# Weight rounding in single operations over two batches, attention units in twos, and a gated block by columns first

## The chip, the core and the metric

The kernel runs on one core of a Trainium2 chip. The metric is the device time of one execution in microseconds; the time before is the median of three runs. The engines work beside each other, each through its own queue in order: TensorE (PE) does matrix products, with its weight loads shown apart as PEld; VectorE (DVE) and ScalarE (ACT) work element by element; GpSimd (POOL) and SyncE (SP) here issue transfers between device memory and the on-chip memories. An engine waits where an operand isn't there or a buffer isn't free.

## The reference

Attention by hash buckets, then a gated feed-forward block on its result:

```
B, H, S, D = 4, 8, 768, 64
q_bits = (einsum('bhsd,dk->bhsk', q, proj) > 0)          # 6 bits
k_bits = (einsum('bhsd,dk->bhsk', k, proj) > 0)
mask   = bucket(q_bits) == bucket(k_bits)                # 2**arange(6)
scores = where(mask, q @ k.T / sqrt(D), -1e9)
attn   = exp(scores - max); attn /= attn.sum(-1) + 1e-9
x      = (attn @ v) as (B*S, H*D) = (3072, 512)
g      = x @ w_gate;  val = x @ w_val                    # 512 -> 1536
out    = (g * sigmoid(g) * val) @ w_out                  # 1536 -> 512
```

q, k, v and proj come as 32-bit floats. The three weight matrices come as 64-bit floats and reach the chip as pairs of 32-bit words.

## The kernel before

**Units.** Two heads of one batch make a pair; there are 16 pairs, four to a batch. A pair has 12 units: two halves of the 768 queries (384 each), and for each half six chunks `c` of 128 keys. `score(u)` (L209) computes, for both heads, keys by queries: two bf16 matmuls of the hash bits, then four instructions of the f32 product, into a tile `sc` with two buffers. The bits are scaled so that equal buckets add zero and others a very large negative number (`OFF` is 2**35). ScalarE takes the exponential (L219) into one of four ring tiles `A`. `attend(u)` (L221) multiplies by v into the accumulator `av`, and VectorE sums the exponentials of the chunks in `acc` (L232, L235). After the sixth chunk ScalarE copies `av` out (L238), and `norm` (L240) sums `acc` over partitions with a matmul into `sum`, takes the reciprocal on VectorE (L251 to L255) and writes a part of `xT`, the input of the gated block.

**Front.** `front(n)` (L170) gives eight steps for a pair: four transposes of q or k on TensorE (`tps`), copied by ScalarE (L182), and four matmuls with `proj2` (`hps`, L187), whose signs VectorE turns to bits (L189), with one more multiply for k (L192). A constant column in `proj2` carries the offset that makes the agreement of all bits sum to zero.

**Weights.** 36 pieces of 128 x 512 doubles are rounded to f32 by integer operations on VectorE: `narrow(i)` (L143) issues seven operations for one piece, through a scratch tile `x`, and then asks GpSimd for the words of piece i + 2 (L141). The first 24 pieces are those of the gate and value weights, in three groups of 512 columns; the last 12 are those of `w_out`.

**Gated block.** When the last normalization of a batch is issued, `push_ffn(b)` (L264) appends 72 closures, here called atoms. `up` (L271) makes 8 matmul instructions into `g` or `val`; for `g` ScalarE does a tanh (L279) and VectorE combines (L280), for `val` VectorE makes `ht` (L285). `down` (L289) does three of twelve steps of the output product into `po` (one buffer), and after the twelfth ScalarE copies it to `o` (L298) and SP writes the rows out. The order is one half of the columns at a time: 24 `up`, then 12 `down`, then the same for the second half.

**Order.** The order on each engine is the order in which the program issues the instructions; nothing is reordered by a planner. One loop (L317) runs over units: `score(u)`, one front step of the next pair where `at >= 2`, one whole `narrow(u)` for the first 36 units, a load of the pair after next at the last unit of a pair, then atoms, of which a credit of 72/44 = 1.64 accrues per unit, then `attend(u - 1)`, then `norm` of unit u - 3 if it closed a half. What is left of the atoms follows the loop.

**Buffers that are shared.** `bank(...)` (L70) gives out two PSUM buffers in turn, for `tps`, `hps`, `sum`, `g` and `val` alike. `po` and `av` have one buffer each, `sc` two of two banks.

Of the kernel before, what the change touches and what calls it, by code (L numbers as in the profile page):

```python
# [17 lines left out]
def kernel(  # L18
# [23 lines left out]
    NF = DF // P  # L42
    PIECE = 512
# [26 lines left out]
    def bank(name):  # L70
        return mm_ps.tile([P, 512], FP32, tag="mm", name=name)
# [5 lines left out]
    def load(n):  # L77
        b, pr = pairs[n]
        for name, src in (("q", q), ("k", k)):
            t = raw.tile([P, NCH, 2, D], FP32, tag=name + "raw", name=name + "raw")  # L80
            for h in range(2):
                nc.sync.dma_start(t[:, :, h, :],
                                  src[b, 2 * pr + h].rearrange("(p c) d -> p c d", c=NCH))
            raws[name, n] = t
        t = raw.tile([P, 2, NCH, D], FP32, tag="vraw", name="vraw", bufs=3)
        nc.sync.dma_start(
            t.rearrange("p h c d -> p h (c d)"),
            v[b, 2 * pr : 2 * pr + 2].rearrange("h (p c) d -> p h (c d)", c=NCH),
        )
        raws["v", n] = t  # L90
# [1 line left out]
    load(0)  # L92


    proj2 = konst.tile([P, P], FP32, tag="proj2", name="proj2")
    nc.vector.memset(proj2, 0.0)
    for o in (0, D):
        nc.sync.dma_start(proj2[o : o + D, o + 1 : o + 1 + NBITS], proj[:, :])
    shift = {}
    for name, one in (("q", -1.0), ("k", 0.25 * NBITS)):  # L100
        t = konst.tile([P, 1], FP32, tag="shift" + name, name="shift" + name)
        nc.vector.memset(t, 0.0)
        for o in (0, D):
            nc.vector.memset(t[o : o + 1 + NBITS], 0.5)
            nc.vector.memset(t[o : o + 1], one)
        shift[name] = t
    ident = konst.tile([P, P], FP32, tag="ident", name="ident")
    make_identity(nc, ident)
    ones = konst.tile([P, D], FP32, tag="ones", name="ones")
# [25 lines left out]
        pieces.append((wo[:, f, :], moe_w_out[f * P : (f + 1) * P, :]))  # L135
    words = {}

    def load_words(i):
        if i < len(pieces):
            words[i] = wraw.tile([P, PIECE, 2], I32, tag="words", name="words")  # L140
            nc.gpsimd.dma_start(words[i].rearrange("p f w -> p (f w)"), pieces[i][1])  # L141

    def narrow(i):  # L143
        t = words.pop(i)
        lo, hi = t[:, :, 0], t[:, :, 1]
        w = pieces[i][0]
        wi = w.bitcast(I32)
        x = wraw.tile([P, PIECE], I32, tag="x", name="x")
        nc.vector.tensor_scalar(wi, hi, scalar1=3, scalar2=0x3FFFFFFF,
                                op0=ALU.logical_shift_left, op1=ALU.bitwise_and)  # L150
        nc.vector.scalar_tensor_tensor(out=wi, in0=hi, scalar=-(1 << 30), in1=wi,
                                       op0=ALU.bitwise_and, op1=ALU.bitwise_or)
        nc.vector.scalar_tensor_tensor(out=wi, in0=lo, scalar=29, in1=wi,
                                       op0=ALU.logical_shift_right, op1=ALU.bitwise_or)
        nc.vector.tensor_scalar(x, lo, scalar1=28, scalar2=1,  # L155
                                op0=ALU.logical_shift_right, op1=ALU.bitwise_and)
        nc.vector.tensor_tensor(wi, wi, x, op=ALU.add)  # L157
        nc.vector.tensor_single_scalar(x, hi, 0x7FFFFFFF, op=ALU.bitwise_and)  # L158
        nc.vector.scalar_tensor_tensor(out=w, in0=x, scalar=float(897 << 20), in1=w,
                                       op0=ALU.is_ge, op1=ALU.mult)  # L160
        load_words(i + 2)

    for i in range(2):
        load_words(i)


    T = {}
# [2 lines left out]
    def front(n):  # L170
# [13 lines left out]
        def hash_bits(name, half):  # L184
            cols = slice(half * HQ, (half + 1) * HQ)
            ps = bank("hps")
            nc.tensor.matmul(ps[:, 0:HQ], proj2, T[name, n][:, cols], start=True, stop=True)  # L187
            o = bits[name, n][:, cols]
            nc.vector.tensor_scalar(o, ps[:, 0:HQ], scalar1=0.0, scalar2=shift[name],  # L189
                                    op0=ALU.is_gt, op1=ALU.subtract)  # L190
# [30 lines left out]
    def attend(u):  # L221
# [12 lines left out]
        elif c > 1:  # L234
            nc.vector.tensor_tensor(acc[n, half], acc[n, half], a[:, :, 0:HQ], op=ALU.add)  # L235
        if c == NCH - 1:
            av[n, half] = att.tile([P, AW], FP32, tag="avs", name="avs")
            nc.scalar.copy(av[n, half], ps[:, 0:AW])  # L238

    def norm(u):  # L240
# [6 lines left out]
        for h in range(2):  # L247
            nc.tensor.matmul(ps[h * D : (h + 1) * D, 0:HQ], ones, t[:, h, :], start=True, stop=True)  # L248
        a = av.pop((n, half))
        r = att.tile([P, HQ], FP32, tag="r", name="r")  # L250
        nc.vector.tensor_scalar(r, ps[:, 0:HQ], scalar1=S * EPS, scalar2=None, op0=ALU.add)  # L251
        nc.vector.reciprocal(r, r)  # L252
        e = att.tile([P, 1], FP32, tag="e", name="e")
# [9 lines left out]

    def push_ffn(b):  # L264
        x = xT.pop(b)
        for half in range(2):
            cols = slice(half * HQ, (half + 1) * HQ)
            hs = []
            now = {}

            def up(f, w, name, x=x, cols=cols, now=now, hs=hs):  # L271
                ps = bank(name)
                for j in range(NJ):
                    nc.tensor.matmul(ps[:, 0:HQ], w[:, j, f * P : (f + 1) * P], x[:, j, cols],  # L274
                                     start=j == 0, stop=j == NJ - 1)

                if name == "g":
                    t = ffn.tile([P, HQ], FP32, tag="t", name="t")
                    nc.scalar.activation(t, ps[:, 0:HQ], AF.Tanh, scale=0.5)  # L279
                    nc.vector.scalar_tensor_tensor(out=t, in0=t, scalar=1.0, in1=ps[:, 0:HQ],  # L280
                                                   op0=ALU.add, op1=ALU.mult)
                    now["t"] = t
                else:
                    ht = hp.tile([P, HQ], FP32, tag="ht", name="ht")
                    nc.vector.scalar_tensor_tensor(out=ht, in0=now["t"], scalar=0.5,  # L285
                                                   in1=ps[:, 0:HQ], op0=ALU.mult, op1=ALU.mult)
                    hs.append(ht)

            def down(i, fs, now=now, hs=hs, half=half):  # L289
                if fs[0] == 0:  # L290
                    now["o"] = po_ps.tile([P, DM], FP32, tag="po", name="po")
                ps = now["o"]
                for f in fs:
                    nc.tensor.matmul(ps, hs[f][:, i * P : (i + 1) * P], wo[:, f, :],  # L294
                                     start=f == 0, stop=f == NF - 1)
                if fs[-1] == NF - 1:
                    o = ffn.tile([P, DM], FP32, tag="o", name="o")
                    nc.scalar.copy(o, ps)  # L298
                    rows = out[b * S : (b + 1) * S, :].rearrange("(p c) m -> p c m", c=NCH)
                    nc.sync.dma_start(rows[:, half * CH + i, :], o)  # L300

            for f in range(NF):
                atoms.append(lambda f=f, up=up: up(f, wg, "g"))
                atoms.append(lambda f=f, up=up: up(f, wv, "val"))
# [9 lines left out]
    rate = 2 * (2 * NF + CH * NF // 3) / (NP * per - 4)  # L314
    credit = 0.0
    steps = []
    for u in range(N + 3):  # L317
        n, at = divmod(u, per)
        if u < N:
            if at == 0 and n + 1 < len(pairs):  # L320
                steps = front(n + 1)
            score(u)
            if at >= 2 and steps:
                steps.pop(0)()
            if u < len(pieces):
                narrow(u)
            if at == per - 1 and n + 2 < len(pairs):
                load(n + 2)
# [42 lines left out]
```

## Time and profile before

| | |
|---|---|
| median of three runs | 1331.69 us (1331.47 to 1332.47) |
| the profiled execution's own time | 1333.82 us |
| its span, first to last instruction | 1331.9 us |
| mean granted TensorE clock | 0.956 |
| TensorE busy | 1224.7 us, 92% |
| VectorE busy | 551.4 us, 41% |
| ScalarE busy | 257.0 us, 19% |
| moved by DMA | 44.74 MB, mean 34 GB/s |

The span runs from the first to the last instruction of the profiled execution; its own time holds some microseconds around it. A busy share is a mean over all stages; TensorE's busy time also holds work done at a lower granted clock. Groups of instructions are shown by source line, engine, operation and tile, with a count and a mean duration. "A <- B" means that A had to wait until B was done. In a timeline the first number is the start in microseconds from the beginning of the span, the second the duration of the merged instructions.

### The profile page before, as it was taken

The numbers are of one execution on the slowest core, as the hardware profiler recorded it, in microseconds if no ns is written. First come the engines' busy times: TensorE is split into PE (matmuls) and PEld (weight loads), VectorE is DVE, ScalarE is ACT, GpSimd is POOL, SyncE is SP. The second block draws the span as 40 slices with busy tenths as digits, with TensorE's granted clock in tenths as the row PEclk, the third lists the DMA queues.
The fourth block names the chain that finished last, engine by engine and source line by source line (L and its number), as shares of the span: only waits on it lengthen the run. The fifth ranks groups of instructions, "written<-read, shape, count | busy, mean of one in ns | idle before, by whom it ended". The sixth has DMA issues, their size and how long they took to land.

```text
span 1331.9 us, 10961 instructions
## 1 busy us (share of the span) xinstructions
PE 1224.7 (92%) x4480; PEld 557.7 (42%) x4480; DVE 551.4 (41%) x840; ACT 257.0 (19%) x409; POOL 20.0 (2%) x46
## 2 busy tenths in 40 slices
PE   5645556999999999999999999999999999999998
PEld 2211112444445443444445443444445443554553
DVE  5999997543224433343224433333224432320110
ACT  2111212312122121312122121312122121110100
POOL 1000000000000000000000000000000000000000
PEclk9875767999999999999999999999999999999999
DMA  8343421000030000300030000300010000000000
GB/s 204 100 130 95 127 98 52 13 0 0 8 80 8 0 0 16 79 1 0 8 86 2 0 1 16 79 0 0 8 52 1 1 0 16 8 0 16 8 0 24
DMA packets 63377, 44.74 MB, mean 34 GB/s; under 512 B 51552, under 2 KB 55648, under 8 KB 63328
## 3 DMA queue, kind: packets, MB, share of 16 engines
q1 hardware_dynamic: 58144, 25.18, 7.3%
q0 software_dynamic: 5184, 18.88, 4.5%
q8 instruction: 35, 0.57, 0.2%
q14 instruction: 14, 0.11, 0.0%
HBM read 37.75 MB, written 6.29 MB: 33 GB/s over the span
## 4 chain that ended last, share of the span: by engine, by line
PE 81%; DVE 15%; issue 2%; DMA 1%; ACT 1%; POOL 0%; ACTq 0%; POOLq 0%; DVEq 0%
PE po L294 19%; PE g L274 19%; PE val L274 18%; PE sc L217 10%; PE av L228 9%; PE hps L187 3%; PE tps L179 2%; DVE acc L235 2%; DVE r L252 2%; PE sum L248 1%; DVE x L158 1%; DVE x L155 1%; DMA words<-in_moe_w_gate_dram 1%; DVE wo L157 1%; DVE wv L157 1%
## 5 line engine op out<-in xcount | busy, mean ns | idle before, releaser
L274 PE MATMUL g<-xT,wg 128*128 128x384 f32 x768 | 265.8, 489 | 1.5 <-DVE kb L189 1.5
L219 ACT ACTIVATE A<-sc 128x768 f32<-128x768 f32 x192 | 155.9, 812 | 567.3 <-PE sc L217 406.9
L294 PE MATMUL po<-wo,ht 128*128 128x512 f32 x576 | 258.9, 597 | 6.9 <-ACT o L298 6.9
L274 PE MATMUL val<-xT,wv 128*128 128x384 f32 x768 | 264.5, 487 | 0.0
L228 PE MATMUL av<-A,vraw 128*64 128x386 f32 x768 | 176.6, 540 | 32.5 <-ACT avs L238 25.2
L280 DVE SCALAR_TENSOR_TENSOR t<-t,g 128x384 f32<-128x384 f32 x96 | 53.2, 555 | 332.5 <-ACT t L279 332.5
L274 PEld LDWEIGHTS g<-xT,wg 128*128 128x128 f32 x768 | 142.7, 190 | 105.7 <-DVE acc L235 6.5
L274 PEld LDWEIGHTS val<-xT,wv 128*128 128x128 f32 x768 | 143.5, 190 | 99.3 <-DVE t L280 5.4
L294 PEld LDWEIGHTS po<-wo,ht 128*128 128x128 f32 x576 | 106.8, 190 | 142.8 <-issue 121.7
L217 PE MATMUL sc<-qT,kT 64*128 64x384 f32 x768 | 164.3, 508 | 0.0
L235 DVE TENSOR_TENSOR acc<-acc,A 128x768 f32<-128x768 f32 x128 | 122.0, 953 | 55.0 <-ACT A L219 53.8
L285 DVE SCALAR_TENSOR_TENSOR ht<-t,val 128x384 f32<-128x384 f32 x96 | 53.1, 554 | 161.8 <-PE val L274 161.8
L279 ACT ACTIVATE t<-g 128x384 f32<-128x384 f32 x96 | 47.2, 491 | 320.7 <-PE g L274 320.7
L228 PEld LDWEIGHTS av<-A,vraw 128*64 128x64 f32 x768 | 39.4, 140 | 143.8 <-issue 103.3
L252 DVE RECIPROCAL r<-r 128x384 f32<-128x384 f32 x32 | 81.7, 2553 | 1.1
L217 PEld LDWEIGHTS sc<-qT,kT 64*128 64x128 f32 x768 | 73.5, 201 | 0.2 <-issue 0.2
L217 PEld LDWEIGHTS <-kb 64*128 64x128 bf16 x384 | 18.5, 93 | 124.4 <-issue 123.1
L217 PE MATMUL sc<-qb,kb 64*128 64x384 bf16 x384 | 67.0, 346 | 0.0
L189 DVE TENSOR_SCALAR qb<-hps,shiftq 128x384 bf16<-128x384 f32 x32 | 19.7, 616 | 86.3 <-PE hps L187 86.3
L248 PE MATMUL sum<-acc,ones 128*64 128x384 f32 x128 | 30.5, 560 | 26.6 <-DVE acc L235 19.6
L187 PE MATMUL hps<-qT,proj 128*128 128x384 f32 x64 | 32.1, 587 | 18.2 <-DVE qb L189 18.2
L298 ACT COPY o<-po 128x512 f32<-128x512 f32 x24 | 14.1, 586 | 122.6 <-PE po L294 122.6
(53 smaller groups left out, 433.1 us busy)
## 6 DMA issues: line engine op xcount, KB each, us to landing
qraw<-in_q_dram SPq DMA_DIRECT2D x32, 192.0 KB, 3.5
words<-in_moe_w_gate_dram POOLq DMA_DIRECT2D x12, 512.0 KB, 3.9
kraw<-in_k_dram SPq DMA_DIRECT2D x32, 192.0 KB, 4.2
vraw<-in_v_dram SPq DMA_DIRECT2D x16, 384.0 KB, 4.4
words<-in_moe_w_val_dram POOLq DMA_DIRECT2D x12, 512.0 KB, 3.8
words<-in_moe_w_out_dram POOLq DMA_DIRECT2D x12, 512.0 KB, 3.6
out_dram<-o SPq DMA_DIRECT2D x24, 256.0 KB, 2.0
proj<-in_proj_dram SPq DMA_DIRECT2D x2, 1.5 KB, 3.3
```

The source lines that it names most:

```text
L187: nc.tensor.matmul(ps[:, 0:HQ], proj2, T[name, n][:, cols], start=True, stop=True)
L217: nc.tensor.matmul(sc[:, h, 0:HQ], x["k", n][rows, ks], x["q", n][rows, qs], start=start, stop=not start)
L219: nc.scalar.activation(ring[u % RING][:, :, 0:HQ], sc[:, :, 0:HQ], AF.Exp, scale=SCALE)
L228: nc.tensor.matmul(ps[h * D : (h + 1) * D, 0:AW], raws["v", n][:, h, c, :], a[:, h, :], start=c == 0, stop=c == NCH - 1)
L235: nc.vector.tensor_tensor(acc[n, half], acc[n, half], a[:, :, 0:HQ], op=ALU.add)
L248: nc.tensor.matmul(ps[h * D : (h + 1) * D, 0:HQ], ones, t[:, h, :], start=True, stop=True)
L252: nc.vector.reciprocal(r, r)
L274: nc.tensor.matmul(ps[:, 0:HQ], w[:, j, f * P : (f + 1) * P], x[:, j, cols], start=j == 0, stop=j == NJ - 1)
L279: nc.scalar.activation(t, ps[:, 0:HQ], AF.Tanh, scale=0.5)
L280: nc.vector.scalar_tensor_tensor(out=t, in0=t, scalar=1.0, in1=ps[:, 0:HQ], op0=ALU.add, op1=ALU.mult)
L285: nc.vector.scalar_tensor_tensor(out=ht, in0=now["t"], scalar=0.5, in1=ps[:, 0:HQ], op0=ALU.mult, op1=ALU.mult)
L294: nc.tensor.matmul(ps, hs[f][:, i * P : (i + 1) * P], wo[:, f, :], start=f == 0, stop=f == NF - 1)
```

## The change

1. Rounding: `narrow` becomes a generator that yields after each operation; `narrow_on(n)` issues n of them. In the first 48 units one operation is issued per unit, and two where `u % 6 == 3`; after that, four behind each atom, until the 252 are used up. The scratch tile `x` is gone: the operations write back into the words. The first two word loads go through SP's queue, behind `load(1)`.
2. Bits: q's hash weights hold the six columns twice, k's once. k's bits are made in one operation, compare and multiply, with constants per partition; the constant column is gone.
3. Units: the first 48 are issued singly, with `attend` one unit behind `score`. From unit 48 on, a step takes two units: the two `attend` calls of the step before (and a `norm` that is due ahead of them), two `score` calls, two front steps, then atoms with a credit of 3.1 per step.
4. The gated block goes by columns first: for each of 12 column blocks both halves' `g` and `val`, then the `down` atoms of both halves. `ht` gets 24 buffers instead of 15; `vraw`, `avs` and `r` get fewer. The load of the pair after next moves one unit forward.

```diff
-    hp = ctx.enter_context(tc.tile_pool(name="hp", bufs=NF + 3))
+    hp = ctx.enter_context(tc.tile_pool(name="hp", bufs=2 * NF))
...
-        t = raw.tile([P, 2, NCH, D], FP32, tag="vraw", name="vraw", bufs=3)
+        t = raw.tile([P, 2, NCH, D], FP32, tag="vraw", name="vraw")
...
+    hash_w = {}
+    for name in "qk":
+        hash_w[name] = konst.tile([P, P], FP32, tag="hash" + name, name="hash" + name)
+        nc.vector.memset(hash_w[name], 0.0)
+        for o in (0, D):
+            for at in (0, NBITS) if name == "q" else (0,):
+                nc.sync.dma_start(hash_w[name][o : o + D, o + at : o + at + NBITS], proj[:, :])
...
+    less_q = column("less_q", 0.5, 0.0)
+    above_k = column("above_k", 0.0, -1.0)
+    times_k = column("times_k", 2.0 * OFF, -OFF)
...
-    def narrow(i):
-        t = words.pop(i)
...
-        x = wraw.tile([P, PIECE], I32, tag="x", name="x")
...
+    def narrow():
+        for i, (w, _) in enumerate(pieces):
+            t = words.pop(i)
+            lo, hi = t[:, :, 0], t[:, :, 1]
...
+            nc.vector.tensor_scalar(lo, lo, scalar1=28, scalar2=1,
+                                    op0=ALU.logical_shift_right, op1=ALU.bitwise_and)
+            yield
+            nc.vector.tensor_tensor(wi, wi, lo, op=ALU.add)
+            yield
+            nc.vector.tensor_single_scalar(hi, hi, 0x7FFFFFFF, op=ALU.bitwise_and)
+            yield
+            nc.vector.scalar_tensor_tensor(out=w, in0=hi, scalar=float(897 << 20), in1=w,
+                                           op0=ALU.is_ge, op1=ALU.mult)
+            load_words(i + 2)
+            yield
...
     for i in range(2):
-        load_words(i)
+        load_words(i, nc.sync)
...
-            nc.vector.tensor_scalar(o, ps[:, 0:HQ], scalar1=0.0, scalar2=shift[name],
-                                    op0=ALU.is_gt, op1=ALU.subtract)
-            if name == "k":
-                nc.vector.tensor_scalar(o, o, scalar1=2.0 * OFF, scalar2=None, op0=ALU.mult)
+            if name == "q":
+                nc.vector.tensor_scalar(o, ps[:, 0:HQ], scalar1=0.0, scalar2=less_q,
+                                        op0=ALU.is_gt, op1=ALU.subtract)
+            else:
+                nc.vector.tensor_scalar(o, ps[:, 0:HQ], scalar1=above_k, scalar2=times_k,
+                                        op0=ALU.is_gt, op1=ALU.mult)
...
-            av[n, half] = att.tile([P, AW], FP32, tag="avs", name="avs")
+            av[n, half] = att.tile([P, AW], FP32, tag="avs", name="avs", bufs=1)
...
-        r = att.tile([P, HQ], FP32, tag="r", name="r")
+        r = att.tile([P, HQ], FP32, tag="r", name="r", bufs=1)
...
+        for f in range(NF):
+            for half in range(2):
+                atoms.append(lambda f=f, half=half: up(f, half, wg, "g"))
+                atoms.append(lambda f=f, half=half: up(f, half, wv, "val"))
         for half in range(2):
...
             for i in range(CH):
                 for f in range(0, NF, 3):
-                    atoms.append(lambda i=i, f=f, down=down: down(i, range(f, f + 3)))
+                    atoms.append(lambda half=half, i=i, f=f: down(half, i, range(f, f + 3)))
...
+    def prepare(u):
+        n, at = divmod(u, per)
+        if at == 0 and n + 1 < len(pairs):
+            steps.extend(front(n + 1))
+        if at == per - 2 and n + 2 < len(pairs):
+            load(n + 2)
+
+    def finish(u):
+        while due:
+            norm(due.pop(0))
+        attend(u)
+        if units[u][2] == NCH - 1:
+            due.append(u)
+
+    alone = NP * per
+    for u in range(alone):
+        prepare(u)
+        score(u)
+        if u % per >= 2 and steps:
+            steps.pop(0)()
+        if u > 0:
+            finish(u - 1)
+        narrow_on(2 if u % 6 == 3 else 1)
+
+    rate = 3.1
     credit = 0.0
...
+    left = [alone - 1]
+    for u in range(alone, N + 2, 2):
+        while left:
+            finish(left.pop(0))
+        if u >= N:
+            while due:
+                norm(due.pop(0))
+            break
+        prepare(u)
+        score(u)
+        score(u + 1)
+        left = [u, u + 1]
+        for _ in range(2):
+            if u % per >= 2 and steps:
+                steps.pop(0)()
         credit = credit + rate if atoms else 0.0
         while atoms and credit >= 1.0:
             credit -= 1.0
             atoms.pop(0)()
-        if 1 <= u < N + 1:
-            attend(u - 1)
-        if u >= 3 and units[u - 3][2] == NCH - 1:
-            norm(u - 3)
+            narrow_on(4)
```

More of the change, by code (lines that the diff above doesn't have):

```diff
@@ L163, with narrow_on @@
+    narrowing = narrow()
+    def narrow_on(n):
+        for _ in range(n):
+            next(narrowing, None)
     for i in range(2):
-        load_words(i)
+        load_words(i, nc.sync)
     T = {}
@@ L265, in push_ffn @@
         x = xT.pop(b)
-        for half in range(2):
[L267 to L304, printed above, removed]
@@ new lines, in down @@
+        def down(half, i, fs):
+            if fs[0] == 0:
+                now["o"] = po_ps.tile([P, DM], FP32, tag="po", name="po")
+            ps = now["o"]
+            for f in fs:
+                nc.tensor.matmul(ps, hs[half][f][:, i * P : (i + 1) * P], wo[:, f, :],
+                                 start=f == 0, stop=f == NF - 1)
+            if fs[-1] == NF - 1:
+                o = ffn.tile([P, DM], FP32, tag="o", name="o")
+                nc.scalar.copy(o, ps)
+                rows = out[b * S : (b + 1) * S, :].rearrange("(p c) m -> p c m", c=NCH)
+                nc.sync.dma_start(rows[:, half * CH + i, :], o)
@@ L313 @@
     per = 2 * NCH
-    rate = 2 * (2 * NF + CH * NF // 3) / (NP * per - 4)
-    credit = 0.0
[L316 to L323, printed above, removed]
+    steps = []
+    due = []
+    def prepare(u):
[20 more added lines that the diff above has]
+    rate = 3.1
+    credit = 0.0
+    left = [alone - 1]
[12 more added lines that the diff above has]
+            if u % per >= 2 and steps:
                 steps.pop(0)()
[L325 to L328, printed above, removed]
         credit = credit + rate if atoms else 0.0
```

66 lines of the change are left out of this document (37 added, 29 removed).

## The prediction

> **What bounds the kernel now.** I read the sliced page first, then busy time by stage, then the waits, then the instructions in order of time around each edit. The clock line and the stages:
>
> ```profile
> PEclk9875767999999999999999999999999999999999
> 16.90:222.70 205.80, 121.11 (x487) 39.62 (x486) 197.29 (x328) 39.68 (x60) 17.99 (x34) 0.72 0.37 108
> 222.70:249.10 26.40, 26.40 (x146) 9.84 (x145) 16.85 (x22) 11.22 (x17) 0.00 (x0) 0.99 0.18 45
> 249.10:394.40 145.30, 144.12 (x533) 66.19 (x531) 49.36 (x70) 29.79 (x48) 0.00 (x0) 1.00 0.05 13
> 1138.10:1331.90 193.80, 186.97 (x530) 99.90 (x528) 30.27 (x52) 15.30 (x30) 0.00 (x0) 1.00 0.02 8
> 249.13 2.75 PE L274 MATMUL g<-xT,wg 128*128 128x384 f32 x8
> ```
>
> Columns of the stages: length, then busy time of PE, PEld, DVE, ACT, POOL, granted clock, DMA share, GB/s. In the first stage (scores 0 to 39, attention alone) VectorE works 197.29 of 205.80 us, 96%, while TensorE has waits and a mean clock of 0.72. In the second (scores 40 to 51, one whole pair's worth, no rounding left) TensorE is busy 26.40 of 26.40 us. From 249.13 us, where the gated block's first product starts, to the end TensorE is the bound at clock 1.00: 144.12 of 145.30 us, and 186.97 of 193.80 us in the tail of 72 atoms alone. So there are two sums: the first stage is paid by VectorE, everything behind it by TensorE and by what makes it wait.
>
> ```profile
> PE sum L248 <- DVE acc L235: 19.6, 3, 8.0
> PE hps L187 <- DVE qb L189: 23.0, 6, 6.6
> PE po L294 <- ACT o L298: 6.9, 10, 0.7
> ```
>
> (Total us, times, longest.) TensorE waited for the attention's VectorE work in the first stage; the 6.9 us on `o` in 10 times are the only repeated wait behind it, 0.69 us each.
>
> **Spreading the rounding: the first stage.** One piece of weights is the stretch from its first operation to the next addition:
>
> ```profile
> 36.54 0.42 DVE L149 TENSOR_SCALAR wv<-words 128x512 int32<-128x512 int32 x1
> 40.58 0.95 DVE L235 TENSOR_TENSOR acc<-acc,A 128x768 f32<-128x768 f32 x1
> L155 DVE TENSOR_SCALAR x<-words 128x512 int32<-128x512 int32 x36 | 15.1, 419 | 0.0
> L151 DVE SCALAR_TENSOR_TENSOR wg<-words,wg 128x512 int32<-128x512 int32 x12 | 8.3, 693 | 0.4
> L157 DVE CUSTOM_DVE_ANT_0 wg<-wg,x 128x1024 uint16<-128x1024 uint16 x12 | 8.3, 694 | 0.4
> L235 DVE TENSOR_TENSOR acc<-acc,A 128x768 f32<-128x768 f32 x128 | 122.0, 953 | 55.0 <-ACT A L219 53.8
> L251 DVE TENSOR_SCALAR r<-sum 128x384 f32<-128x384 f32 x32 | 17.7, 554 | 40.0 <-PE sum L248 39.9
> L252 DVE RECIPROCAL r<-r 128x384 f32<-128x384 f32 x32 | 81.7, 2553 | 1.1
> L254 DVE TENSOR_SCALAR e<-avs 128x1 f32<-128x1 f32 x32 | 3.1, 96 | 0.0
> L255 DVE SCALAR_TENSOR_TENSOR xT<-avs,e,r 128x384 f32<-128x384 f32 x32 | 19.8, 619 | 1.1
> L189 DVE TENSOR_SCALAR qb<-hps,shiftq 128x384 bf16<-128x384 f32 x32 | 19.7, 616 | 86.3 <-PE hps L187 86.3
> L280 DVE SCALAR_TENSOR_TENSOR t<-t,g 128x384 f32<-128x384 f32 x96 | 53.2, 555 | 332.5 <-ACT t L279 332.5
> L279 ACT ACTIVATE t<-g 128x384 f32<-128x384 f32 x96 | 47.2, 491 | 320.7 <-PE g L274 320.7
> ```
>
> Seven operations take 40.58 - 36.54 = 4.04 us. The edit drops the scratch tile: L155 and L158 now write into the loaded words, every second word, and L157 reads its second operand so. L155 already reads such a stride at 419 ns and L151 at 693, so I leave these at their price (bounds 0.42, and 0.69 if writing at a stride costs what two operands cost). L157 handles 1024 halves in 694 ns; if the stride breaks their pairing, 512 more elements at (953 - 555)/384 = 1.04 ns (L235 against L280) make it 1.22 us. Bounds 0.69 and 1.22; I take 0.83, nearer the strided reads that cost nothing. A piece is then 4.18 us, one operation 0.60.
>
> VectorE per pair of heads (12 units): 10 additions at 0.953 = 9.5; two normalizations of 0.554 + 2.553 + 0.096 + 0.619 = 3.82, 7.6; four bit operations at 0.616, 2.5, the separate k multiply being gone; 14 rounding operations (one per unit and one more twice) at 0.60, 8.4. Sum 28.0 us, against TensorE's 26.4 from the second stage. So this stage stays VectorE's, narrowly, at 28.0/12 = 2.33 us a unit, where it had been 205.8/40 = 5.15. The queues can slide against each other: an exponential waits for the addition four units back, so VectorE's lag behind a normalization (3.82 + 0.62 against a unit of TensorE) is below that slack. A wait that moves is the sum of the denominators, now one unit after its last addition instead of two; I add 2 us in all for it. 52 scores at 2.33 = 121.3, less four units without rounding at the end, -2.4, plus 2, from 16.9 + 0.5: the first gated product starts at 138.3 us, not 249.1. **Gain 110.8 us.**
>
> The 0.5 is the start: four more copies of `proj` are issued on SP ahead of the next loads, and the first two word loads come behind them.
>
> ```profile
> 8.23 1.15 SPq L98 DMA_DIRECT2D proj<-in_proj_dram  x2
> words<-in_moe_w_gate_dram POOLq DMA_DIRECT2D x12, 512.0 KB, 3.9
> ```
>
> Two issues took 1.15 us, so up to 2.3 us if the first bit matmul waits for all; against it two 512 KB loads no longer run beside the first q and k. I bound it by -2 and +2.3. Later words are fetched on POOL, 3.9 us after issue, with at least seven rounding operations of VectorE in between (4.2 us, and more with what is put between them): covered, and if not, 0.5 us in each of 28 pieces. `vraw` with two buffers makes SP wait for the last attend of the pair before, one step of two units; behind it in SP's queue are only output rows, whose tile is double and written every fourth atom. I take nothing, also for `avs` and `r` with one buffer, used once in six units.
>
> **Units in twos: what TensorE saves behind 138 us.**
>
> ```profile
> 16.91 0.34 PE L217 MATMUL sc<-qb,kb 64*128 64x384 bf16 x2
> 17.73 0.33 PE L217 MATMUL sc<-qb,kb 64*128 64x384 bf16 x2
> 612.46 0.34 PE L217 MATMUL sc<-qb,kb 64*128 64x384 bf16 x2
> 613.37 2.85 PE L274 MATMUL g<-xT,wg 128*128 128x384 f32 x8
> 618.73 0.87 PE L228 MATMUL av<-A,vraw 128*64 128x386 f32 x4
> 619.53 0.34 PE L217 MATMUL sc<-qb,kb 64*128 64x384 bf16 x2
> 623.50 0.87 PE L228 MATMUL av<-A,vraw 128*64 128x386 f32 x4
> 624.20 0.81 PE L248 MATMUL sum<-acc,ones 128*64 128x384 f32 x4
> 624.95 0.34 PE L217 MATMUL sc<-qb,kb 64*128 64x384 bf16 x2
> 256.65 2.58 PE g L274 x8
> ```
>
> Read from start to start: scores take 0.91 us before a gated product (612.46 to 613.37), 0.82 before other scores; av takes 0.80 before scores, 0.70 before a product of its own shape (623.50 to 624.20); the sum 0.75. Two atoms between scores and av take 5.36 us (613.37 to 618.73) where the chain has 2.58 for one in a row: 0.20 for changing over. Two units side by side save 0.10 + 0.09 = 0.19 us, in 24 steps of a batch 4.6; change-overs fall from 44 (1.64 atoms a unit) to 23.5 (3.1 a step), 4.1. Three batches: **-26 us**.
>
> **What it costs: the two banks.** Transposes, bits, sums and both gated products share two PSUM banks. Two front steps now stand next to each other, and the first atom behind them takes the bank of the first.
>
> ```profile
> 620.45 0.55 PE L179 MATMUL tps<-ident,qraw 128*128 128x128 f32 x3
> 620.61 0.81 ACT L219 ACTIVATE A<-sc 128x768 f32<-128x768 f32 x1 [3.86 <-PE sc L217]
> 620.83 2.75 PE L274 MATMUL g<-xT,wg 128*128 128x384 f32 x8
> 621.32 0.47 ACT L182 COPY qT<-tps 128x384 f32<-128x384 f32 x1
> 265.64 0.91 PE L187 MATMUL hps<-qT,proj 128*128 128x384 f32 x2
> 266.39 2.74 PE L274 MATMUL g<-xT,wg 128*128 128x384 f32 x8
> ```
>
> A transpose takes TensorE 0.38 us (620.45 to 620.83); its copy ends at 621.79, 1.34 us after its start, because ScalarE first does the second exponential. Until now a product in the other bank hid this. Now the second transpose covers only 0.38, so TensorE waits 1.34 - 0.76 = 0.58, with the signal 0.65 us: two such steps in each of 11 pairs, **+14.3**. Two bit matmuls (0.75 and about 0.65) just cover their bit operation of 0.62; but in the step that also normalizes, VectorE does 3.82 and an addition of 0.95 first. From the start of the sum: bits done at 0.75 + 0.1 + 3.82 + 0.95 + 0.62 = 6.2, wanted at 0.75 + 1.50 (av) + 1.73 (scores) + 1.4 = 5.4; 0.8 in 11 pairs, **+8.8**. Gated output groups of four atoms now meet their successor inside a step two times in three: 12 + 5 waits on `o` for 10, at 0.69, **+4.8**.
>
> **Rounding under the first batch's gated block.** 196 operations are left, four behind each of 49 atoms, in 16 steps. VectorE per atom: 0.555 + 4 x 0.60 = 2.95 against 2.58. Three atoms: the first gated operation starts 2.58 + 0.1 + 0.49 = 3.2 us in, the last rounding ends at 3.2 + 3 x 2.95 = 12.0, TensorE's at 7.74. The attention part lets VectorE catch up: in steps without bits the next gated operation isn't late. In the step with bits: 12.0 + 1.9 (two additions) + 0.62 = 14.5 against 7.74 + 3.23 + 1.4 = 12.4, a wait of 2.1. With bits and normalization: 12.0 + 3.82 + 0.95 + 0.62 = 17.4 against 13.1, 4.3, of which 0.8 is counted. Three pairs: 3 x 5.6 = **+17**. Bounds: 0 if the slack takes the lag, 16 x 2.1 = 34 if every step waits as the one with bits does. Weights are ready in time: gate columns of group two are rounded after 14 atoms and used by the 17th.
>
> **The sum.** 1331.9 - 110.8 - 26 + 14.3 + 8.8 + 4.8 + 17 = 1240.0 us of span. The profiled execution took 1333.82, 1.9 more than its span, and the median of the runs shown is 1331.69, 2.1 below it: 1240.0 + 1.9 - 2.1 = **1240 us**.
>
> [...]
>
> **The rivals.**
>
> *The banks don't bind* (22%): if ScalarE copies earlier than I put it, and VectorE's small operations catch up, 14.3 + 8.8 + 17 fall away: 1200. For it, TensorE waited for no bank behind 249 us; against it, transposes never stood in twos there.
>
> *The add loses its pairs* (12%): 1.22 for 0.83 us. 0.8 us more per pair in 4.3 pairs, 3.4; and 0.69 us in each step of the first batch, which adds to the three loaded steps of 2.7 pairs, 5.6: 1249. [...]
>
> *VectorE decides both stages* (9%): the lag isn't absorbed, the first stage takes 33 us a pair (28.0 + 5 of waits) and rounding steps cost a whole loaded step more: 1240 + 4.3 x 5 + 14 = 1275.
>
> *The clock doesn't come up* (4%, slower): with waits in every unit or step TensorE stays where the first stage had it. The two stages hold 26.4 x 52/12 = 114 and 16 x 12.4 = 198 us of TensorE's work (3.1 atoms 8.0, change-over 0.20, av 1.50, scores 1.73, a sixth of four transposes, four bit matmuls and two sums 0.97); as I cost them they last 121 + 220. At a clock of 0.65, between the 5 and the 7 of the sliced line, they take 480, so 1240 + 139 = 1379. It decides from a clock of 312/(341 + 92) = 0.72 on: below it, the kernel is slower than before. For it: 0.72 is the first stage's mean. Against: with VectorE 1.06 times TensorE the waits are short, and in 222.7 to 249.1 the clock was 0.99.
>
> *It doesn't do what it says* (3%): units in the first stage are held by the order of sum, copy and scores, not by VectorE's amount; then 205.8 us stay and the +18.9 of the later stages come on top: 1351.
>
> **How the numbers follow.** 50% for 1240, with 1222 to 1258 its own range (the 17 from 0 to 34, the start +/-2). 1198 takes in the first rival, 1262 the second; the other three and the edges of the first two cases, about a fifth, are left outside. Faster by over 0.2% (2.7 us, about what a measurement can tell) is all but the last two, 0.93; slower those two, 0.06; 0.01 between.
>
> **What would show it.** First gated product near 138 us, clock about 1.0 in the stage before, VectorE busy above 90% there. Two adjacent scores 0.82 apart. Waits of TensorE for the copies L182 in 22 places near 0.65 us, for the bits in the step that normalizes; the longest three in the first batch. In-place operations at 0.42, the add near 0.83. I am wrong if the first product starts after 160 us, or if a later batch (296 us each before, (1138.1 - 249.1)/3) changes by over 5 us.

## The result

| | before | after |
|---|---|---|
| median | 1332.06 us | 1228.42 us (1227.17 to 1228.82) |
| ratio | | 0.9221, 95% interval 0.9205 to 0.9237 |
| profiled execution, its span | 1333.82, 1331.9 us | 1227.17, 1225.4 us |
| mean granted clock | 0.956 | 0.997 |
| first score | 16.91 us | 13.50 us |
| first gated product | 249.13 us | 131.84 us |

The forecast was 1240 us, from 1198 to 1262. The profile after, in busy time by stage (length, PE, PEld, DVE, ACT, POOL, granted clock, DMA share, GB/s): attention alone, the first batch of the gated block, the second.

```profile
13.50:131.80 118.30, 114.59 (x631) 42.09 (x630) 103.67 (x147) 52.27 (x78) 4.36 (x8) 1.00 0.36 94
131.84:444.72 312.88, 293.64 (x1121) 143.70 (x1121) 205.01 (x333) 64.05 (x103) 14.11 (x26) 0.99 0.22 64
444.72:742.20 297.48, 290.33 (x1120) 142.49 (x1120) 102.40 (x137) 64.02 (x103) 0.00 (x0) 1.00 0.09 22
```

In the first stage TensorE is now busy 114.59 of 118.30 us at clock 1.00. VectorE, busy 96% of that stage before, is busy 103.67 us, 88%. In the first batch VectorE has 205.01 us of work, in the second 102.40; the difference is the moved rounding, and the first batch is 15.4 us longer. What TensorE waited for (total us, times, longest):

```profile
PE val L295 <- DVE qb L211: 10.9, 6, 3.4
PE po L316 <- ACT o L320: 9.8, 14, 0.7
PE g L295 <- DVE qb L211: 7.8, 5, 3.5
PE tps L200 <- DMA qraw<-in_q_dram: 5.2, 1, 5.2
PE val L295 <- ACT qT L203: 4.8, 9, 0.5
PE sum L271 <- DVE acc L258: 3.0, 4, 0.8
PE g L295 <- ACT qT L203: 4.5, 9, 0.5
```

All but one of these rows are the waits that the prediction named: the bits behind the reciprocal and the rounding (18.7 us in 11 times), the transposes' copies (9.3 in 18), `o` (9.8 in 14) and the sum (3.0). The row of `qraw` is the first load. Single operations, the first four after and the last two before (these have line, shapes and count first, then total us and mean ns):

```profile
L166 DVE TENSOR_SCALAR words<-words 128x512 int32<-128x512 int32 x36 | 15.4, 426 | 0.8
L171 DVE TENSOR_SCALAR words<-words 128x512 int32<-128x512 int32 x36 | 15.2, 422 | 0.0
L169 DVE CUSTOM_DVE_ANT_0 wg<-words,wg 128x1024 uint16<-128x1024 uint16 x12 | 8.3, 691 | 0.3
L214 DVE TENSOR_SCALAR kb<-hps,above_k,times_k 128x384 bf16<-128x384 f32 x32 | 21.5, 672 | 3.9 <-PE hps L208 3.6
L189 DVE TENSOR_SCALAR kb<-hps,shiftk 128x384 bf16<-128x384 f32 x32 | 19.7, 614 | 39.9 <-PE hps L187 39.9
L192 DVE TENSOR_SCALAR kb<-kb 128x384 bf16<-128x384 bf16 x32 | 8.3, 260 | 1.1
```

Writing back into every second word costs nothing that shows (426 and 422 ns, for the 419 of L155 before), and the add takes 691 ns with a strided operand, for 694 before. The one-operation k bits take 672 ns, where two took 614 and 260.

The batches of the gated block in the timelines (us). The column "first" is the start of the first gated product; each batch lasts from its first gated product to that of the next, and "rest" is the fourth batch, from its first gated product to the end of the span:

```
                      first   batch 1  batch 2  batch 3  rest
before                249.13   299.4    299.4    290.2   193.8
after                 131.84   312.9    297.5    288.9   194.3
rounding in pieces    249.43   299.0    297.5    288.8   194.4
single units          128.84   306.7    299.0    291.2   194.3
first operation only  131.88   299.7    297.5    288.9   194.3
halves first          131.44   349.0    297.1    287.2   193.4
front steps apart     130.88   310.0    294.1    285.1   194.3
tail of norm later    131.84   300.5    296.1    286.3   194.4
groups of o in steps  131.74   311.7    295.7    285.6   194.3
words on GpSimd       135.46   316.4    297.5    288.8   194.5
all three mends       130.73   293.9    289.6    279.2   194.3
single, tail later    128.58   304.3    299.0    291.2   194.3
```

In the two rows with single units the gated block starts one unit earlier, behind 51 scores where the others have 52. The work of that unit, about 2 us, lies in batch 3 there, and so the columns "first" and "batch 3" of these two rows aren't for the same work as in the others.

### The profile page after: what moved, and what is told of

Its sections match the earlier page's. It is cut to its first block, busy times and chain, and to the rows that moved or that the text cites. A ratio compares the mean times of both kernels' runs of the same rounds, so it can differ in the third digit from the quotient of the medians.

```text
span 1225.4 us, 10930 instructions
## 1 busy us (share of the span) xinstructions
PE 1174.4 (96%) x4480; PEld 569.4 (46%) x4480; DVE 540.5 (44%) x814; ACT 257.7 (21%) x409; POOL 19.3 (2%) x44
## 4 chain that ended last, share of the span: by engine, by line
PE 82%; DVE 12%; ACT 4%; issue 1%; DMA 0%; SPq 0%; ACTq 0%
PE po L316 21%; PE g L295 20%; PE val L295 19%; PE sc L240 9%; PE av L251 8%; DVE r L275 3%; ACT A L242 2%; DVE acc L258 2%; PE hps L208 2%; PE sum L271 2%; PE tps L200 1%; DVE qb L211 1%; DVE acc L255 1%; ACT o L320 1%; DVE xT L278 1%
## 5 line engine op out<-in xcount | busy, mean ns | idle before, releaser
L240 PE MATMUL sc<-qT,kT 64*128 64x384 f32 x768 | 155.1, 482 | 0.0
L251 PE MATMUL av<-A,vraw 128*64 128x386 f32 x768 | 149.4, 499 | 0.3 <-ACT A L242 0.2
L251 PEld LDWEIGHTS av<-A,vraw 128*64 128x64 f32 x768 | 47.2, 136 | 83.9 <-issue 82.7
L240 PEld LDWEIGHTS sc<-qT,kT 64*128 64x128 f32 x768 | 68.9, 189 | 16.4 <-issue 16.4
L274 DVE TENSOR_SCALAR r<-sum 128x384 f32<-128x384 f32 x32 | 17.7, 554 | 123.4 <-PE sum L271 122.9
L240 PE MATMUL sc<-qb,kb 64*128 64x384 bf16 x384 | 63.8, 329 | 0.0
L211 DVE TENSOR_SCALAR qb<-hps,less_q 128x384 bf16<-128x384 f32 x32 | 19.6, 614 | 45.0 <-PE hps L208 45.0
L261 ACT COPY avs<-av 128x386 f32<-128x386 f32 x32 | 15.4, 482 | 82.3 <-PE av L251 82.3
```

Of the source, the lines that this page charges most:

```text
L240: nc.tensor.matmul(sc[:, h, 0:HQ], x["k", n][rows, ks], x["q", n][rows, qs], start=start, stop=not start)
L251: nc.tensor.matmul(ps[h * D : (h + 1) * D, 0:AW], raws["v", n][:, h, c, :], a[:, h, :], start=c == 0, stop=c == NCH - 1)
```

## The experiments

Each is an edit of the changed kernel. Times are medians; a ratio is to the kernel before on the same chip.

**Rounding in whole pieces again.**

```diff
-        narrow_on(2 if u % 6 == 3 else 1)
+        narrow_on(7 if u < len(pieces) else 0)
...
             atoms.pop(0)()
-            narrow_on(4)
```

> All of the change stays, only the rounding goes back to whole pieces of seven operations in the first 36 units, none behind the atoms. Theory (VectorE's rounding set the first stage): the first gated product falls back to 13.5 + 205.8 + 26.4 = about 245 us, the first batch of the gated block loses its rounding and takes 297.5 us like the later ones; span 245 + 297.5 + 297.5 + 288.9 + 194.3 = 1323, time 1325, 0.3 to 0.7% below the kernel before. Rival (pairs of units, column order or the k bits carry a good part of the gain, 26 us or more): 1300 or less.

Measured 1330.78 us, ratio 0.9987 (0.9978 to 0.9996). Without the spread rounding the rest of the change is worth 0.13%. The first gated product is back at 249.43 us:

```profile
13.60:223.00 209.40, 110.09 (x490) 38.05 (x490) 197.27 (x322) 39.65 (x60) 18.09 (x34) 0.76 0.39 113
17.31 0.43 DVE L157 TENSOR_SCALAR wg<-words 128x512 int32<-128x512 int32 x1 [2.94 <-DMA words<-in_moe_w_gate_dram]
```

VectorE is busy 197.27 us again and TensorE's clock 0.76. It came out nearly 6 us above the expectation. Some 4 us of that are the first gated product, put at about 245 us: the earlier start is worth little when VectorE sets the pace. Its first rounding begins at 17.31 us, when the words have landed, against 17.84 before, and from there to the first gated product it takes 232.1 against 231.3 us. Another 1.5 us are the first batch, 299.0 us where 297.5 was expected. The rival, that pairs or order carry a good part, is out.

**Units singly behind unit 48.**

```diff
-    rate = 3.1
+    rate = 1.55
...
-    for u in range(alone, N + 2, 2):
+    for u in range(alone, N + 1):
...
+        if u < N:
+            prepare(u)
+            score(u)
+            if u % per >= 2 and steps:
+                steps.pop(0)()
...
+        finish(u - 1)
```

> Behind unit 48 the units are issued singly again (1.55 atoms a unit, one front step a unit), the rounding stays spread. Theory (pairs save some 7 us of change-overs a batch and give back 5 to 6 in waits for the two banks and for o): a later batch takes 299 instead of 297.5 us, the first one between 304 and 314; time 1222 to 1233. Rival one, pairs are a clear gain: 1245 or more. Rival two, pairs cost more than they save: 1215 or less.

Measured 1222.07 us, 0.9175 (0.9160 to 0.9191), at the lower edge of the expectation: 6.4 us faster than the pairs. The times of both rivals are out, though with the rounding counted the pairs as built do cost more than they save. In the second batch pairs win 1.5 us, as the expectation had it. In the first they lose 6.2, because single units hide most of the rounding: TensorE's waits for bits in that batch fall from 14.1 us to about 2, and 3.3 us of waits behind `r` come instead. Pairs also lose 3.0 us ahead of the first gated product and win 2.3 in the third batch; about 2 us of both is the unit that lies elsewhere (under the table above). TensorE's waits in this run:

```profile
PE po L316 <- ACT o L320: 7.6, 11, 0.7
PE val L295 <- DVE r L274: 2.1, 3, 0.8
PE g L295 <- DVE r L274: 1.2, 2, 1.0
PE g L295 <- DVE qb L211: 0.9, 1, 0.9
PE val L295 <- DVE qb L211: 0.9, 1, 0.9
```

**Rounding under the gated block cut to its first operation.** From the ninth piece on six of seven rounding operations are left out, in unchanged places.

```diff
+            thin = i >= 8
...
             yield
+            if thin:
+                for _ in range(5):
+                    yield
+                load_words(i + 2)
+                yield
+                continue
```

> From the ninth piece on only the first of the seven rounding operations is issued, in the same places, so those weights are wrong; VectorE has 168 operations less under the first batch. Theory (in the first batch 14 us of waits for the bits come from rounding queued ahead of them on VectorE): these waits fall to some 2 us, the first batch from 312.9 to about 299 us, time 1214 to 1217. Rival one (the normalization alone holds the bits up): 1226 to 1228. Rival two (rounding costs more than the waits show, by bandwidth or clock): 1205 or less.

Measured 1213.89 us, 0.9113 (0.9099 to 0.9127): 14.5 us less, and the first batch falls from 312.9 to 299.7, 13.2; both rivals are out. The 168 operations had kept VectorE busy for 93 us (205.0 to 111.7 us in that batch) and cost TensorE 13. The waits for the bits in that batch fall by 10.7 us, from 14.1 to 3.4, and the other 2.6 are a slow product that the changed kernel has there (last section). What is left for bits, in all batches, is the normalization's part:

```profile
PE val L302 <- DVE qb L218: 5.6, 5, 1.3
PE g L302 <- DVE qb L218: 2.4, 3, 0.8
```

**By halves first, eight operations behind an atom.**

```diff
-        for f in range(NF):
-            for half in range(2):
+        for half in range(2):
+            for f in range(NF):
...
-            narrow_on(4)
+            narrow_on(8)
```

> The gated block goes by halves first again, so its columns are needed twice as fast: eight rounding operations behind each atom instead of four. Theory (column order is what makes the rounding thin enough to hide): for the first 24.5 atoms VectorE has 196 x 0.577 + 24.5 x 0.55 + 8 x 3.3 = 153 us of work against TensorE's 99; 54 more, less the 14 of waits there now; time about 1268. Rival (the slack of the queues takes it): 1228 to 1238.

Measured 1260.92 us, 0.9466 (0.9452 to 0.9480). It is slower by 32 us than with columns first, where 40 was expected, and the rival is out. In the stretch that holds the rounding, 159 us where 153 was expected, VectorE is busy 89%, TensorE 76% at a granted clock of 0.88.

```profile
131.44:290.40 158.96, 120.38 (x416) 58.86 (x418) 142.05 (x250) 23.18 (x38) 13.92 (x26) 0.88 0.29 90
```

(Length, then PE, PEld, DVE, ACT, POOL, granted clock, DMA share, GB/s, as above.) So the column order pays by halving the pace at which weights are needed; the run changes order and pace together, since one asks for the other. The first batch is 36.1 us longer than with columns first; the rest of the kernel is 3 to 4 us shorter. One wait for `o` less (0.7 us), one for the bits less in the third batch (1.0) and an earlier first product (0.4) are some 2 us of it; what the others are isn't settled.

**Front steps apart.**

```diff
         prepare(u)
+        if u % per >= 2 and steps:
+            steps.pop(0)()
         score(u)
         score(u + 1)
         left = [u, u + 1]
-        for _ in range(2):
-            if u % per >= 2 and steps:
-                steps.pop(0)()
+        if u % per >= 2 and steps:
+            steps.pop(0)()
```

> In a step of two units the first front step goes between the two attends and the two scores, the second stays ahead of the atoms. Theory (the first atom waits for the bank of the first of two neighbouring transposes): the 18 waits for the copy of qT, 0.59 us each with the pipeline's part, are gone, 10.6 us; one more change-over of about 0.1 in 44 places gives back up to 4.4; time 1218 to 1223. Waits for bits unchanged. Rival (ScalarE's order, not the neighbourhood, makes the wait; it moves to the scores): 1227 to 1233.

Measured 1216.68 us, 0.9134 (0.9122 to 0.9147): 11.7 us less, 1.3 us below the expectation. No wait for a copy of `qT` is left, and the rival is out. This is the wait as it stands in the changed kernel:

```profile
443.36 0.55 PE L200 MATMUL tps<-ident,qraw 128*128 128x128 f32 x3
443.75 0.49 PE L200 MATMUL tps<-ident,kraw 128*128 128x128 f32 x3
444.19 0.47 ACT L203 COPY qT<-tps 128x384 f32<-128x384 f32 x1
444.72 2.85 PE L295 MATMUL g<-xT,wg 128*128 128x384 f32 x8 [0.48 <-ACT qT L203]
```

The copy ends at 444.66, 1.30 us after its transpose began; the second transpose covers 0.39, and the product starts 0.06 after the copy. From the second transpose to the product it is 0.97 us where one transpose to the next is 0.39: 0.58 lost, of which the row shows 0.48 as a wait. Besides these waits, 9.3 us, those for the bits fell too, from 18.7 to 16.4 us, which the expectation had left unchanged; the extra change-overs cost less than their bound of 4.4.

**The tail of a normalization behind the front steps.**

```diff
+        def rest():
-        nc.vector.reciprocal(r, r)
+            nc.vector.reciprocal(r, r)
...
+        rests.append(rest)
...
+        settle()
         credit = credit + rate if atoms else 0.0
```

> From unit 48 on the last three operations of a normalization (reciprocal, e, xT) are issued behind the front steps of the step instead of ahead of its attends. Theory (the bits wait for the reciprocal on VectorE): the waits of 3.4 us in the first batch fall to about 1, those of 0.8 to 1.0 later are gone; 7 + 5 = 12 us less, 1214 to 1219. Rival (the reciprocal then delays the gated block's own operations and TensorE waits there): 1225 to 1232.

Measured 1210.42 us, 0.9086 (0.9073 to 0.9098): 18.0 us less, 12.4 of them in the first batch. The expectation was 12, and the rival is out. The three operations, 3.27 us of which the reciprocal takes 2.55, had stood ahead of the bits. TensorE's waits for the bits fall from 18.7 to 4.3 us in all, and the slow product in the first batch (2.6 us, last section), which the expectation had not counted, is gone. With the rounding in place the first batch is now only 0.8 us longer than it was with the rounding cut to its first operation (300.5 and 299.7), and 4.3 us of waits for bits are left in it. So most of what rounding cost TensorE was paid through this one place in VectorE's queue.

```profile
PE g L299 <- DVE qb L211: 2.9, 3, 1.3
PE val L299 <- DVE qb L211: 1.4, 1, 1.4
```

**A whole output group to a step.**

```diff
-    rate = 3.1
+    rate = 4 * NF / 18
...
-        credit = credit + rate if atoms else 0.0
+        if not atoms:
+            credit = 0.0
+        elif kinds[0]:
+            credit = NF // 3
+        else:
+            credit = credit + rate
```

(`kinds` holds 0 for an up atom and 1 for an output atom; a step stops before the first output atom.)

> A step issues 48/18 = 2.67 up atoms, and in the output part four atoms, one whole group, so that groups meet only across steps. Theory: the 9 waits for o ahead of the tail, 0.69 us each, are gone, 6.2 us, and the rounding meets more attention per atom, 0 to 5 us; 1217 to 1222. Rival (the copy of o then waits behind the exponentials or the attends): 1226 to 1229.

Measured 1220.99 us, 0.9163 (0.9151 to 0.9176): 7.4 us less, within the expectation. Waits for `o` fall from 14 to the 5 of the tail, 6.2 us, and the rival is out. The waits for the two shared banks stay as they were, 27.7 us in 30 times for 28.0 in 29. What makes the remaining 1.2 us isn't shown.

```profile
PE po L317 <- ACT o L321: 3.6, 5, 0.7
```

**First words on GpSimd's queue.**

```diff
-        load_words(i, nc.sync)
+        load_words(i)
```

> The first two word loads go back to GpSimd's queue at the start. Theory (they ran beside the first q and k, so the first transpose began at 9.1 instead of 5.2 us): the first score comes 3 to 4 us later, 1231 to 1233. Rival (the start is set by the six copies of proj on SP): 1228 to 1229.

Measured 1231.59 us, 0.9250 (0.9237 to 0.9262), 3.2 us more. The first transpose is back at 9.00 us and the first score at 17.12:

```profile
9.00 0.87 PE L200 MATMUL tps<-ident,qraw 128*128 128x128 f32 x3 [9.00 <-DMA qraw<-in_q_dram]
17.12 0.34 PE L240 MATMUL sc<-qb,kb 64*128 64x384 bf16 x2
```

So the two word loads had held up the first q and k. The issues of `proj` hardly matter: with them and with the words on GpSimd's queue the first score comes 0.2 us later than in the kernel before. The profiled execution of this run is 3 us above its median, and its first batch is 3.5 us longer than that of the changed kernel: see the last section.

**All three mends.** Front steps apart, tail later, groups in steps.

> The three mends together: the first front step between attends and scores, the last three operations of a normalization behind the front steps, 2.67 up atoms or one whole output group to a step. Alone they took 11.7, 18.0 and 7.4 us off. Theory (three separate waits, each with its own cause): they add up, 1228.4 - 37 = 1191, within 4 us. Rival (they share the same lag of VectorE in the first batch): the first batch cannot fall much below the 299 it has without rounding, so 1198 to 1204.

Measured 1189.85 us (1189.54 to 1190.47), 0.8933 (0.8920 to 0.8945). The three add up, 38.6 us against 37.1. The rival is out: the first batch, 293.9 us, goes below the 299.7 that it had with the rounding cut to its first operation. TensorE's waits behind the first gated product:

```profile
PE po L321 <- ACT o L325: 3.6, 5, 0.7
PE val L300 <- DVE qb L211: 3.2, 3, 1.2
```

**Single units with the tail later.** The edits of single units and of the tail together, with the tail behind the next unit's front step.

> Units singly behind unit 48, as in the run of single units, with the last three operations of a normalization issued behind the front step of the next unit. Theory (with its waits taken away, a pair of units saves TensorE 22 to 26 us over three batches; single units have few waits to lose): later batches 297 to 299 us, the first 299 to 304, time 1212 to 1218, so 22 to 28 above the pairs with all three mends (1189.9). Rival (pairs save little even then, and the mends made the whole difference): 1200 or less.

Measured 1219.65 us, 0.9154 (0.9142 to 0.9167), 1.7 us above the expectation and 29.8 above the mended pairs; the rival is out. Single units had few waits to lose (2.4 us) and in later batches gain nothing. Of the 29.8 us, 4.1 are waits for `o` (11 against 5 times) and 3.3 waits for `r`; against these stand 3.2 us of waits for the bits that only the mended pairs have:

```profile
PE po L320 <- ACT o L324: 7.7, 11, 0.7
PE val L299 <- DVE r L274: 2.1, 3, 0.8
PE g L299 <- DVE r L274: 1.2, 2, 1.0
```

That leaves some 26 us. The change-overs that pairs avoid are the likely part of it; this is what remains after the waits, and no run measured the change-overs by themselves. The first batch is 5.3 us longer than the second. Of this 3.3 us are waits, and TensorE is busy 1.8 us longer (299.47 against 297.68) with the same products; why isn't settled.

## Why the prediction was right

It was 11.6 us high, inside its range, and its direction and size held for the reasons given. The first of its six terms was sized too small, the other five too large, so the errors cancel in part. In spans of the two profiled executions (these lie 1.8 us above the median before and 1.3 below it after, so that the medians differ by 103.6 us where the spans differ by 106.5):

| term | forecast | measured | from |
|---|---|---|---|
| first gated product earlier | -110.8 | -117.3 | 249.13 - 131.84 |
| change-overs saved by pairs | -26 | -21.1 | what remains, not measured alone |
| wait for the first transpose's bank | +14.3 | +9.3 | rows of `qT` |
| bits behind the normalization | +8.8 | +6.5 | 8 waits left without rounding, 8.0, less 1.5 before |
| groups meeting on `o` | +4.8 | +2.9 | 9.8 - 6.9 |
| rounding under the first batch | +17 | +13.2 | 312.9 - 299.7 |
| sum | -91.9 | -106.5 | 1331.9 to 1225.4 |

The change-overs are a remainder, then. Against single units the same subtraction of named waits gives 22 us for the kernel as built and 26 us for the mended one, so the size holds, but no run measured them alone.

**The first stage.** The mechanism was right (whole pieces bring 249 us back), two sizes were off. The start was bounded at -2 to +2.3, taken at +0.5, and came 3.4 us earlier: the two word loads beside the first q and k were priced at 2 us at most, and they set the start. The first transpose began at 5.24 us instead of 9.14 (the first line is from before):

```profile
9.14 0.87 PE L179 MATMUL tps<-ident,qraw 128*128 128x128 f32 x3 [9.14 <-DMA qraw<-in_q_dram]
5.24 0.87 PE L200 MATMUL tps<-ident,qraw 128*128 128x128 f32 x3 [5.24 <-DMA qraw<-in_q_dram]
13.50 0.34 PE L240 MATMUL sc<-qb,kb 64*128 64x384 bf16 x2
131.84 2.85 PE L295 MATMUL g<-xT,wg 128*128 128x384 f32 x8 [0.48 <-ACT qT L203]
```

And "this stage stays VectorE's, narrowly" is wrong: from first score to first gated product it took 118.3 us, 97% of them TensorE's, against 120.9. The forecast held 118.9 us of VectorE's work, a pair's 28.0 us scaled to 52 units less 2.4. Scaling gave 8.7 normalizations and 43.3 additions, where the stage has 8 and 41, and the rounding went in at 0.60 us an operation for 0.577; with the true counts and durations the operations last 112.7 us end to end. They also overlap a little in the trace, so that VectorE is busy for only 103.67 us: in the profile of before an addition of 0.95 us starts at 40.58 and the next operation at 41.45, 0.87 us later. The add at 0.83 was wrong too; it is 0.69. So of the signs named, "VectorE busy above 90% there" failed (88%), while two adjacent scores do stand 0.82 us apart (441.64 and 442.46).

**The clock** came up as forecast, 1.00 in a stage that had 0.72. So the rival on the slower side is out, and so is the one in which units were held by their order.

**The banks.** Both waits are where they were put. Those for the copies are 0.52 us each in the rows against 0.65, those for the bits 1.0 (in the run with the rounding cut) against 0.8. But they come 18 and 8 times and not 22 and 11: a third of the atoms are output atoms, whose product goes to `po` and takes no bank. I had counted every pair. The waits for `o` came 14 times for 17. "The banks don't bind" is out: the runs with the front steps apart and the tail later took those 11.7 and 18.0 us away.

**Rounding under the first batch.** The six places are the ones named (bits, and bits with normalization, in three pairs); four of them:

```profile
158.33 2.85 PE L295 MATMUL g<-xT,wg 128*128 128x384 f32 x8 [1.31 <-DVE qb L211]
174.78 2.85 PE L295 MATMUL val<-xT,wv 128*128 128x384 f32 x8 [3.14 <-DVE qb L211]
253.36 2.85 PE L295 MATMUL val<-xT,wv 128*128 128x384 f32 x8 [3.40 <-DVE qb L211]
334.76 5.49 PE L295 MATMUL g<-xT,wg 128*128 128x384 f32 x8 [3.52 <-DVE qb L211]
```

The waits are 1.3 to 1.4 us where 2.1 was forecast, and 3.1 to 3.5 where 4.3 was. VectorE's lag had been summed at 0.60 us an operation and without overlap, which goes that way; no run separates the two. The 17 us held waits alone. Of the 13.2 measured, 10.7 are waits (14.1 less the 3.4 left without rounding) and 2.6 the slow product behind one of them, which isn't in the forecast's sum. VectorE didn't decide the first batch.

**The add's pairs.** The rival in which a strided operand breaks the pairing of halves, 1.22 us, is out: with it the add on 1024 halves takes 691 ns, as long as before (694) and as an operation with two operands on 512 words (L151, 693).

**What I undervalued.** That pairs as built were no gain: my own terms gave -26 + 14.3 + 8.8 + 4.8 = +1.9, and with rounding +17 more; the measured balance against single units is +6.4 (single units pay for rounding too: their first batch is 7.7 us longer than their second). The sum said so without my saying it.

## What to carry to other kernels

In this kernel the work that was moved under another stage cost what stood behind it in its engine's queue, not its own duration: rounding that kept VectorE busy for 93 us cost 13, and most of that went when the last three operations of a normalization, 3.27 us, were issued after, not before, the operations that free a shared bank. When two producers that alternate on two buffers are put side by side, count who takes the first buffer next and what is left to cover its release: here 18 waits, 9.3 us. And before a first stage is costed, look at which transfers run beside the first loads: two word loads there made the first transpose begin at 9.00 instead of 5.24 us.

## What the runs showed that was not expected

Whether TensorE's clock drops behind a wait of 3.1 to 3.5 us differs from one profiled execution to another. Of the three long waits in the profile after, one of 3.52 us was followed by half the clock (start and end of the stretch first, the clock third from the end):

```profile
330.00:334.00 4.00, 1.24 (x4) 0.38 (x2) 3.93 (x5) 0.66 (x1) 0.00 (x0) 0.94 0.36 131
334.00:338.00 4.00, 3.24 (x5) 1.85 (x6) 1.29 (x3) 0.00 (x0) 0.00 (x0) 0.50 0.00 0
```

The product behind it took 5.49 us where those behind the other two took 2.85. In the profiled execution with the first words on GpSimd, which differs from the changed kernel only in the queue of these two loads, all three were followed by a slow product, at almost the same waits (granted clock 0.97 from 135.46 to 352.00 us, for 0.98 from 131.84 to 348.00 in the profile after):

```profile
178.40 4.54 PE L295 MATMUL val<-xT,wv 128*128 128x384 f32 x8 [3.14 <-DVE qb L211]
258.66 5.49 PE L295 MATMUL val<-xT,wv 128*128 128x384 f32 x8 [3.41 <-DVE qb L211]
342.99 4.54 PE L295 MATMUL g<-xT,wg 128*128 128x384 f32 x8 [3.52 <-DVE qb L211]
```

That is 1.7 + 2.6 + 1.7 = 6.0 us instead of 2.6, and 3.4 of the 3.5 us by which that first batch is longer. In the run with whole output groups all three long waits, 3.25, 3.39 and 3.12 us, were also followed by a slow product (4.51, 4.52 and 4.54 us). The length of the wait alone doesn't tell the two cases apart: a slow product follows waits of 3.12 and 3.14 us in these runs, and none follows those of 3.14 and 3.40 us in the profile after. What tells them apart isn't shown. The ends of products are modelled in the profile, so this stays open. In the kernels in which these waits are gone (tail later and all three mends, where the longest wait for bits is 1.4 and 1.2 us) the mean clock is 1.00.
